# A new order of weight preparation at the hand-over from attention to the first expert layer

## The chip, the cores and the metric

One Trainium2 chip, one core. The metric is the device time of one execution in microseconds (us). The kernel before took 1001.23 us, the median of 3 runs (1000.52 to 1001.75). Its profile is of one more execution.

## The reference

Three layers run one after the other in float32.

```python
# attention: q, k, v are (4, 8, 576, 64); q and k are rotated first
scores = q_rot @ k_rot.T / sqrt(64)
attn = exp(scores - max); attn = attn / (sum(attn) + 1e-9)
x = (attn @ v).transpose(0, 2, 1, 3).reshape(2304, 512)
# first expert layer: w_in (512, 2048), w_out (2048, 512), float64
h = maximum(x @ w_in, 0)
x = (h * h) @ w_out
# second layer: 8 experts, each token goes to one
logits = x @ w_gate + modality_bias[modality_id]
e = argmax(logits); gate = softmax(logits)[e]
out = gate * (maximum(x @ w1[e], 0) @ w2[e])
```

## The kernel before

Every float32 matmul is done as three passes over a high and a low part of each operand. TensorE (PE) does the matmuls, VectorE (DVE), ScalarE (ACT) and GpSimd (POOL) make the parts, and SyncE (SP) issues all plain transfers, in order. Each engine carries out its instructions in the order in which the program lists them; an instruction that waits holds up all behind it on its engine.

Attention works on 16 pairs of heads. A table, `PLAN`, gives each step of a pair a due time, and the steps of all pairs are sorted by due time, 18 units further on per pair. A second table, `TAIL`, puts steps of the next layer into the same sorted list: the due times of that table are counted from the end of the 16th pair. The prefixes in `TAIL` name the steps: `wd` loads half a weight tile of the first expert layer (512 KB as 64-bit words) into one of 4 buffers `wraw`; `wx` (lines 518 to 520) takes its magnitude and turns its low words into floats on ACT; `wy` (524, 525) clamps and shifts on DVE; `wz` (529) merges both on POOL; `wb` (533) puts the sign back on DVE; `wh` (546) makes the high part on ACT; `wl` (549) makes the low part on POOL or DVE. The magnitude lives in one of 4 buffers of tag `t2`, named `wmag`. `xs0` to `xs3` load the first 512 tokens, `cl` and `setup` load the routing constants and prepare them (670 to 680).

The first expert layer goes over 5 blocks of up to 512 tokens, 16 slices of the hidden layer each, which makes 80 steps n. `m1` is the first matmul of a step (12 instructions at line 696, into a PSUM bank of tag `b`, of which there are 4). Then `re` (relu, 702) and `sq` (square, 706) run on ACT, `gg` and `gl` (710 and 714: the square again, and its low part) on DVE, and `m2` is the second matmul (12 instructions at line 730). `m1` runs two steps ahead of `m2`. Up to `m20` the order comes from `TAIL`; after it a loop over steps takes over. In block 0 the loop also prepares the other weights: `slot(i)` works on three half tiles at once, an even and an odd slot per step. An even half tile holds a slice of w_in, an odd one a slice of w_out. Weights stay in SBUF, so that blocks 1 to 4 prepare none. From block 1 on the logits are summed on DVE (`lg_dve`, line 742).

The tile `r` of relu comes from the tag `kr`, which has two buffers. In this kernel the first two tiles of that tag are `c_lt` and `wg_sb`, two of the routing constants.

Of the kernel before, what the change touches and what calls it, by code (L numbers as in the profile page):

```python
# [9 lines left out]
F32 = mybir.dt.float32  # L10
F32R = mybir.dt.float32r
BF16 = mybir.dt.bfloat16
I32 = mybir.dt.int32
# [8 lines left out]
B, H, S, D = 4, 8, 576, 64  # L22
NTOK, DM, DFF = B * S, H * D, 2048
E, EF = 8, 1024
# [10 lines left out]
def f32(ap):  # L35
    return ap.bitcast(F32)
# [129 lines left out]
}  # L166


# [316 lines left out]
class Weights:  # L485

    def __init__(self, nc, wio, pool):
        self.nc, self.wio, self.pool, self.extra, self.ring = nc, wio, pool, None, None
        self.w, self.raw, self.mag = {}, {}, {}

    def t2(self, shape, dt, name):
        return self.pool.tile(shape, dt, name=name, tag="t2", bufs=4)
# [37 lines left out]

    def sign(self, i):
        mag = self.mag[i]
        self.nc.vector.scalar_tensor_tensor(out=mag, in0=self.words(i)[:, :, 1], scalar=-2 ** 31, in1=mag,
                                            op0=ALU.bitwise_and, op1=ALU.bitwise_or)
        self.raw.pop(i)

# [15 lines left out]
def experts(tc, wts, ps, xT, rD, wexp, mod, wg, mb, cst, ident, yD, out):  # L552
    nc = tc.nc
    with ExitStack() as ctx:
# [3 lines left out]
        W, t2 = wts.w, wts.t2  # L558
# [4 lines left out]
        def kr(shape, dt, name):  # L563
            return sb.tile(shape, dt, name=name, tag="kr", bufs=2)

        def small(shape, dt, name):
            return sb.tile(shape, dt, name=name)
# [4 lines left out]
        xs, rs, gs, hs, yp, ysb, wgb, yts, tables = {}, {}, {}, {}, {}, {}, [], {}, {}  # L572
        raws, rbs = {}, {}

        def xload(b, ks):
            t0, n = BLOCKS[b]
            for k in ks:
                x = sb.tile([128, 2, n], F32R, name="xs", tag="xs", bufs=5)
                nc.sync.dma_start(out=f32(x), in_=xT[k, :, :, t0:t0 + n])
                xs[b, k] = x  # L580
# [45 lines left out]

        c_io8 = small([128, E], F32, "c_io8")
        c_io128 = small([128, 128], F32, "c_io128")
        c_lt = kr([128, 128], F32, "c_lt")
        c_id = small([128, NT], F32, "c_id")  # L630
        wg_sb = kr([128, 4, E], F32, "wg_sb")
        mb_sb = small([128, 2, E], F32, "mb_sb")
        mod_sb = small([128, NT, 2], I32, "mod_sb")

        def cload():
            o = 0
            for t, n in ((c_io8, E), (c_io128, 128), (c_lt, 128), (c_id, NT)):
                nc.sync.dma_start(out=t, in_=cst[:, o:o + n])
                o += n
            nc.sync.dma_start(out=wg_sb, in_=wg[0:DM].rearrange("(k p) e -> p k e", p=128))  # L640
            nc.sync.dma_start(out=mb_sb, in_=mb.rearrange("m e -> (m e)").partition_broadcast(128))
            nc.sync.dma_start(out=mod_sb, in_=mod.bitcast(I32).rearrange("(j p w) -> p j w", p=128, w=2))
# [24 lines left out]
        six = small([128, NCOL], I32, "six")  # L667

        def setup():
            nc.vector.tensor_copy(out=lt_b, in_=c_lt)  # L670
            nc.vector.memset(one_b, 1.0)
            nc.vector.memset(cum[:, 0], 0.0)
            nc.vector.tensor_copy(out=wg_s[:, :, 0:E], in_=wg_sb)
            nc.vector.tensor_tensor(out=wg_s[:, :, E:2 * E], in0=wg_sb, in1=f32(wg_s[:, :, 0:E]), op=ALU.subtract)
            nc.vector.tensor_copy(out=modf[:, 1], in_=mod_sb[:, :, 0])
            nc.vector.tensor_scalar(out=modf[:, 0], in0=modf[:, 1], scalar1=-1.0, scalar2=1.0, op0=ALU.mult, op1=ALU.add)
            for m, t in enumerate((bias, tmp3)):
                nc.vector.tensor_tensor(out=t, in0=modf[:, m].unsqueeze(2).to_broadcast([128, NT, E]),
                                        in1=mb_sb[:, m].unsqueeze(1).to_broadcast([128, NT, E]), op=ALU.mult)
            nc.vector.tensor_tensor(out=bias, in0=bias, in1=tmp3, op=ALU.add)  # L680
# [367 lines left out]
        pre, mid, post = {}, {}, {}  # L1048

        def at(d, n, *fs):  # L1050
            d.setdefault(n, []).extend(fs)
# [5 lines left out]
        for b in range(NB):  # L1057
            if b:
                q = NFC * b
                for k in range(4):  # L1060
                    if b == 1:
                        at((mid, pre)[k % 2], q - 6 + (k + 1) // 2, lambda b=b, k=k: xraw(b, k))
                        at(mid, q - 12 + k, lambda b=b, k=k: xrec(b, k))
                        e = nc.gpsimd if k < 2 else nc.vector
# [51 lines left out]
        def second(m):  # L1116
# [5 lines left out]
            if f == EFC - 1:  # L1122
                for t in ts:
                    finish(s, t)

        units = [(first, mm2, n) for n in range(N)] + [(emm1, second, m) for m in range(M0, M1)]
        yield dict(xs=lambda k: xload(0, [k]), cl=lambda _: cload(), setup=lambda _: setup(), m1=mm1, re=relu, sq=square,
                   gg=square_v, gl=rest, m2=mm2)
        wts.ring = ctx.enter_context(tc.tile_pool(name="w", bufs=1, reuse_waits="tile"))
        for q, (_, second_, n) in enumerate(units):  # L1130
            if q < NU - LA:
# [32 lines left out]
@with_exitstack  # L1164
def tile_attention_moe(ctx, tc, qx, kx, v, wio, wexp, mod, wg, mb, tabq, tabk, eye, cst, out):
    nc = tc.nc
    const = ctx.enter_context(tc.tile_pool(name="const", bufs=1))
    pool = ctx.enter_context(tc.tile_pool(name="wts", bufs=1))
    dram = ctx.enter_context(tc.tile_pool(name="scratch", bufs=1, space=DRAM))
    ident = const.tile([128, 128], F32, name="ident")  # L1170
    xT = dram.tile([4, 128, 2, NTOK], F32, name="xT")
    yD = dram.tile([NTOK, DM], F32, name="yD")
    rD = dram.tile([NP, 9, 128], F32, name="rD")
    wts = Weights(nc, wio, pool)
    ps = ctx.enter_context(tc.tile_pool(name="ps", bufs=1, space=PSUM))
    run = experts(tc, wts, ps, xT, rD, wexp, mod, wg, mb, cst, ident, yD, out)
    fs = dict(wd=wts.load, wx=wts.absolute, wy=wts.clamp, wz=wts.merge, wb=wts.sign, wh=wts.high)

    def tail(name, eng):
        if name == "open":  # L1180
            fs.update(next(run))
        elif name in fs:
            fs[name](0)
        elif name[0:2] == "wl":
            wts.low(int(name[2:]), nc.vector if eng == "V" else nc.gpsimd)
        else:
            fs[name[0:2]](int(name[2:]))

    with tc.manual_schedule():
        attention(tc, qx, kx, v, tabq, tabk, ident, eye, xT, rD, ps, tail)  # L1190
        next(run, None)
# [84 lines left out]
```

## Time and profile before

| | |
|---|---|
| time, median of 3 runs | 1001.23 us |
| time of the profiled execution | 998.48 us |
| its span, first to last instruction | 996.6 us |
| PE busy | 913.4 us (92% of the span) |
| DVE busy | 689.3 us |
| ACT busy | 532.3 us |
| POOL busy | 378.6 us |

Times of the trace are counted from the start of the span. Attention ends and the first expert layer begins at 317.69 us. A row of a timeline gives the start, the busy time (from the first to the last of the merged instructions), the engine, the line of the kernel, the operation, what it writes and reads, the count, and in brackets how long the engine had been idle before it and what ended the wait. SPq rows are transfers, from issue. [...]

### The profile page before, as it was taken

To read this page: it belongs to the slowest core of one execution; us is meant where nothing else is said; L and a number is where in the kernel's file an instruction comes from. 1 tells how busy PE (TensorE), PEld (TensorE's weight loads), DVE (VectorE), ACT (ScalarE), POOL (GpSimd) and SP (SyncE) were. 2 spreads that over 40 slices of the span, in tenths; PEclk is the share of its full clock that TensorE was granted. 3 is DMA by queue.
4 is the path that set the end of the run, shared out by engine and by line. 5 is a ranking of instruction groups with operands and counts; after the bars stand their busy time and mean duration, and the time that the engine had idled before them with its cause. 6 is when DMAs were issued, how large, how long until landed. Compare 5 with 4: busy or idle time off the path is not lost. (4 is left out here: it accounts for less than half of the span.)

```text
span 996.6 us, 15017 instructions
## 1 busy us (share of the span) xinstructions
PE 913.4 (92%) x5210; PEld 789.6 (79%) x5210; DVE 689.3 (69%) x1253; ACT 532.3 (53%) x1090; POOL 378.6 (38%) x292
## 2 busy tenths in 40 slices
PE   1888889999999598889999999999999999999996
PEld 0778888988888366668878887888888889999995
DVE  5889988989896699958555754665374766666650
ACT  3788888889897476631233223222434345555551
POOL 6778887878753466714001200200010123212011
PEclk9999999999999799999999999999999999999998
DMA  7556557565755445443003100300133258776630
GB/s 239 150 156 189 170 143 202 147 197 177 203 144 150 128 149 189 149 161 112 1 1 127 43 1 1 106 1 1 43 124 109 76 165 251 233 238 224 210 107 33
DMA packets 55714, 130.83 MB, mean 131 GB/s; under 512 B 11968, under 2 KB 16592, under 8 KB 55632
## 3 DMA queue, kind: packets, MB, share of 16 engines
q1 hardware_dynamic: 52592, 120.10, 39.6%
q0 software_dynamic: 3040, 9.70, 2.7%
q8 instruction: 43, 0.70, 0.3%
q14 instruction: 39, 0.32, 0.1%
HBM read 97.12 MB, written 19.21 MB: 117 GB/s over the span
## 5 line engine op out<-in xcount | busy, mean ns | idle before, releaser
L696 PE MATMUL h<-xs,w 128*128 128x512 f32 (+1 forms) x720 | 163.7, 373 | 9.7 <-POOL w L549 9.7
L702 ACT ACTIVATE r<-h 128x512 f32<-128x512 f32 (+1 forms) x80 | 44.4, 555 | 236.1 <-PE h L696 219.8
L696 PEld LDWEIGHTS h<-xs,w 128*128 128x128 f32 x720 | 125.5, 188 | 40.1 <-POOL w L549 14.1
L710 DVE SCALAR_TENSOR_TENSOR h<-h,r 128x512 f32<-128x512 f32 (+1 forms) x80 | 51.5, 644 | 125.2 <-ACT r L702 124.9
L730 PE MATMUL y<-w,gh 128*128 128x512 f32 x432 | 135.8, 396 | 0.0
L272 PE MATMUL sc<-kh,q 128*128 128x288 f32 (+2 forms) x336 | 98.5, 328 | 37.2 <-ACT kh L194 20.7
L288 ACT ACTIVATE e<-sc,nmx 128x576 f32<-128x576 f32 x144 | 107.0, 744 | 27.5 <-DVE nmx L277 27.1
L277 DVE TENSOR_REDUCE nmx<-sc 128x1 f32<-128x576 f32 x144 | 106.6, 750 | 17.2 <-PE sc L272 15.1
L967 DVE TENSOR_TENSOR w<-eraw,w 128x1024 fp32r<-128x1024 f32 x64 | 78.3, 1223 | 33.8 <-ACT w L966 33.6
L272 PEld LDWEIGHTS sc<-kh,q 128*128 128x128 f32 x336 | 62.7, 196 | 47.2 <-issue 24.1
L199 DVE TENSOR_TENSOR et<-b,et 128x512 fp32r<-128x512 f32 (+1 forms) x160 | 93.8, 624 | 8.0 <-ACT et L194 6.0
L330 PE MATMUL b<-ident,e 128*128 128x128 f32 x640 | 89.1, 277 | 9.6 <-DVE et L199 3.9
L730 PEld LDWEIGHTS y<-w,gh 128*128 128x128 f32 x432 | 80.2, 188 | 17.5
L272 PE MATMUL sc<-kl,q 128*128 128x288 f32 (+2 forms) x336 | 90.9, 305 | 0.0
L330 PEld LDWEIGHTS b<-ident,e 128*128 128x128 f32 x640 | 72.7, 141 | 18.3 <-PE b L321 5.2
L730 PE MATMUL y<-w,gl 128*128 128x512 f32 x216 | 84.9, 393 | 0.0
L194 ACT ACTIVATE et<-b 128x512 fp32r<-128x512 f32 (+1 forms) x160 | 82.7, 561 | 1.3 <-PE b L330 0.8
L364 PE MATMUL b<-et,vs 128*128 128x288 f32 x512 | 78.4, 295 | 0.1
L1012 PEld LDWEIGHTS h<-ye,w 128*128 128x128 f32 x576 | 75.1, 189 | 3.9
L615 POOL TENSOR_TENSOR xraw<-xraw,rbs 128x512 f32<-128x512 f32 (+1 forms) x12 | 15.7, 1310 | 159.6 <-DMA rbs<-xT 93.6
L1012 PE MATMUL h<-ye,w 128*128 128x256 f32 x576 | 76.3, 283 | 0.0
L1035 PE MATMUL y<-w,ge 128*128 128x512 f32 x288 | 75.3, 397 | 0.0
(216 smaller groups left out, 1832.4 us busy)
## 6 DMA issues: line engine op xcount, KB each, us to landing
eraw<-wexp SPq DMA_DIRECT2D x64, 512.0 KB, 3.5
wraw<-wio SPq DMA_DIRECT2D x32, 512.0 KB, 4.0
rawq<-qx SPq DMA_DIRECT2D x15, 576.0 KB, 5.0
rawk<-kx SPq DMA_DIRECT2D x15, 576.0 KB, 6.5
xT<-xo SPq DMA_DIRECT2D x24, 288.0 KB, 6.1
kh<-kh SPq DMA_DIRECT2D x45, 144.0 KB, 2.3
vraw<-v SPq DMA_DIRECT2D x16, 320.0 KB, 6.3
q<-ql SPq DMA_DIRECT2D x32, 144.0 KB, 3.9
```

Of the source, the lines that this page charges most:

```text
L194: nc.scalar.activation(out=out, in_=in_, func=ACTF.Copy)
L199: on[eng].tensor_tensor(out=out, in0=in0, in1=f32(hi), op=ALU.subtract)
L272: nc.tensor.matmul(out=o[:, x:x + w], lhsT=q[:, hd, q0:q0 + 128], rhs=k[:, hd, y:y + w], start=(n == 0), stop=(n == len(ops) - 1))
L277: nc.vector.tensor_reduce(out=m, in_=sc(p, j)[:, :, 0:HS], axis=AX.XY, op=ALU.max, negate=True)
L288: nc.scalar.activation(out=e(p)[:, o:o + S].rearrange("p (a b) -> p a b", a=2), in_=sc(p, j)[:, :, 0:HS], func=ACTF.Exp, bias=live[p, f"nm ...
L330: nc.tensor.transpose(t[:, i * 128:(i + 1) * 128], x[:, o:o + 128], ident)
L364: nc.tensor.matmul(out=o, lhsT=lhsT.rearrange("p a b -> p (a b)"), rhs=rhs, start=(c == 0 and i == 0), stop=(c == 4 and i == 1))
L696: nc.tensor.matmul(out=h, lhsT=w[:, a, k * 128:(k + 1) * 128], rhs=xs[b, k][:, c], start=(k == 0 and i == 0), stop=(k == 3 and i == 2))
L730: nc.tensor.matmul(out=yp[t], lhsT=g[a][:, t * 128:(t + 1) * 128], rhs=w[:, c, 512:1024], start=(f == 0 and i == 0), stop=(f == NFC - 1 an ...
L967: nc.vector.tensor_tensor(out=w[:, 1], in0=r, in1=f32(w[:, 0]), op=ALU.subtract)
L1012: nc.tensor.matmul(out=h, lhsT=w[:, a, k * 128:(k + 1) * 128], rhs=x[:, c], start=(k == 0 and i == 0), stop=(k == 3 and i == 2))
L1035: nc.tensor.matmul(out=yp[s, t], lhsT=g[a][:, t * 128:(t + 1) * 128], rhs=w[:, c, 512:1024], start=(f == 0 and i == 0), stop=(f == EFC - 1 ...
```

## The change

Three things change. The due times of the second half of `TAIL` are new, `wl4` to `wl7` move from POOL to DVE, and `m10` to `m20` with what follows each of them are interleaved with the weight steps. The loading and the preparation of the routing constants leave `TAIL` for steps 13 and 17 of the loop; `c_lt` and `wg_sb` now lie in one buffer of tag `t2` instead of two of tag `kr`. And in the loop the sign step of an odd half tile writes into a PSUM bank of tag `b`, which its high and low parts then read.

```diff
@@ TAIL @@
...
-    "wd6": (-138.181, "D"), "wl1": (-93.230, "P"), "wd7": (-88.464, "D"), "xs0": (-84.177, "D"),
...
-    "m10": (1204.840, "T"), "m11": (1293.864, "T"), "re0": (1305.121, "A"), "wh7": (1325.671, "A"),
...
+    "wd6": (-138.181, "D"), "wz4": (-103.400, "P"), "wl1": (-101.000, "P"), "wl2": (-100.500, "P"),
...
+    "wy8": (-70.950, "V"), "wz8": (-70.940, "P"), "m10": (-70.930, "T"), "m11": (-70.920, "T"), "re0": (-70.910, "A"),
...
@@ class Weights @@
     def sign(self, i):
         mag = self.mag[i]
-        self.nc.vector.scalar_tensor_tensor(out=mag, in0=self.words(i)[:, :, 1], scalar=-2 ** 31, in1=mag,
+        if self.bank and i % 2:
+            self.mag[i] = self.bank([128, 512], "wbank").bitcast(I32)
+        self.nc.vector.scalar_tensor_tensor(out=self.mag[i], in0=self.words(i)[:, :, 1], scalar=-2 ** 31, in1=mag,
                                             op0=ALU.bitwise_and, op1=ALU.bitwise_or)
@@ experts @@
-        c_lt = kr([128, 128], F32, "c_lt")
...
-        wg_sb = kr([128, 4, E], F32, "wg_sb")
...
+        passing = []
...
         def cload():
-            o = 0
+            o, t = 0, t2([128, 160], F32, "c_t")
+            c_lt, wg_sb = passing[:] = t[:, 0:128], t[:, 128:160].rearrange("p (k e) -> p k e", e=E)
...
         def setup():
+            c_lt, wg_sb = passing
...
+        at(mid, 13, cload)
+        at(mid, 17, setup)
-        yield dict(xs=lambda k: xload(0, [k]), cl=lambda _: cload(), setup=lambda _: setup(), m1=mm1, re=relu, sq=square,
-                   gg=square_v, gl=rest, m2=mm2)
+        yield dict(xs=lambda k: xload(0, [k]), m1=mm1, re=relu, sq=square, gg=square_v, gl=rest, m2=mm2)
+        wts.bank = bank
```

Before, on ACT, from the last evacuation of attention (`xo`) to the first relu (`r`); the words in brackets name the queues or engines that a row waits for:

```order
L194 ACTIVATE xo<-b 128x288 [waits PE_49] x2
L519 ACTIVATE wmag<-wraw 128x512 [waits Pool_49]
L520 ACTIVATE wraw<-wraw 128x512
L546 ACTIVATE wf<-wmag 128x512 [waits DVE_49] x2
L519 ACTIVATE wmag<-wraw 128x512 [waits DMAHW6_49,Activation_49,Pool_49]
L520 ACTIVATE wraw<-wraw 128x512
L519 ACTIVATE wmag<-wraw 128x512 [waits DMAHW7_49,Pool_49]
L520 ACTIVATE wraw<-wraw 128x512
L519 ACTIVATE wmag<-wraw 128x512 [waits DMAHW0_49,Pool_49]
L520 ACTIVATE wraw<-wraw 128x512
L702 ACTIVATE r<-h 128x512 [waits DMAHW2_49,DVE_49,PE_49]
```

After, the same stretch on ACT (line numbers from 530 on are 2 or 3 higher):

```order
L548 ACTIVATE wf<-wmag 128x512
L194 ACTIVATE xo<-b 128x288 [waits PE_49]
L519 ACTIVATE wmag<-wraw 128x512 [waits DMAHW5_49,Pool_49]
L520 ACTIVATE wraw<-wraw 128x512
L194 ACTIVATE xo<-b 128x288 [waits PE_49]
L548 ACTIVATE we<-wmag 128x512 [waits DVE_49,Activation_49]
L519 ACTIVATE wmag<-wraw 128x512 [waits DMAHW7_49,Activation_49]
L520 ACTIVATE wraw<-wraw 128x512
L705 ACTIVATE r<-h 128x512 [waits PE_49]
L709 ACTIVATE gh<-r 128x512 [waits Activation_49]
L548 ACTIVATE we<-wmag 128x512 [waits DVE_49]
```

Of the three magnitude pairs that stood between the last `xo` and the first relu, `wx7`, `wx8` and `wx9`, one is left there (`wx8`); the relu waits for PE alone and no longer for a DMA queue and DVE.

Before, on SP, from the last sums of attention (`rD`) to the first weight load of the new layer:

```order
L305 DMA rD<-rs 9x128 [waits DMAHW5_49,Activation_49]
L391 DMA xT<-xo 64x2x576 [waits DMAHW6_49,Activation_49]
L391 DMA xT<-xo 64x2x576 [waits DMAHW7_49]
L638 DMA c_io_3981<-cst 128x8 [waits DMAHW0_49]
L638 DMA c_io_3982<-cst 128x128 [waits DMAHW1_49]
L638 DMA c_lt<-cst 128x128 [waits DMAHW2_49]
L638 DMA c_id<-cst 128x18 [waits DMAHW3_49]
L640 DMA wg_sb<-wg 128x4x8 [waits DMAHW4_49]
L641 DMA mb_sb<-mb 128x16 [waits DMAHW5_49]
L642 DMA mod_sb<-mod 128x18x2 [waits DMAHW6_49]
L496 DMA wraw<-wio 128x512 [waits DMAHW7_49,DVE_49]
```

After, SP from one store of sums earlier:

```order
L305 DMA rD<-rs 9x128 [waits Activation_49]
L496 DMA wraw<-wio 128x512 [waits DMAHW7_49,DVE_49,Pool_49]
L496 DMA wraw<-wio 128x512 [waits DMAHW0_49,DVE_49]
L391 DMA xT<-xo 64x2x576 [waits DMAHW1_49,Activation_49]
L391 DMA xT<-xo 64x2x576 [waits DMAHW2_49]
L581 DMA xs<-xT 128x2x512 [waits DMAHW3_49,PE_49]
L581 DMA xs<-xT 128x2x512 [waits DMAHW4_49,DVE_49,PE_49]
L581 DMA xs<-xT 128x2x512 [waits DMAHW5_49]
L581 DMA xs<-xT 128x2x512 [waits DMAHW6_49]
L305 DMA rD<-rs 9x128 [waits DMAHW7_49,Activation_49]
L496 DMA wraw<-wio 128x512 [waits DMAHW0_49,DVE_49]
```

Two weight loads, `wd8` and `wd9`, now stand ahead of the token loads `xs`, where before they stood behind seven loads of constants.

Before, on DVE, one step of block 0:

```order
L710 SCALAR_TENSOR_TENSOR h<-h,r 128x512 [waits Activation_49]
L714 TENSOR_TENSOR gl<-h,gh 128x512 [waits DVE_49,PE_49,Activation_49]
L524 TENSOR_SCALAR wmag<-wmag 128x512 [waits Activation_49]
L525 TENSOR_SCALAR wmag<-wmag 128x512 [waits DVE_49]
L533 SCALAR_TENSOR_TENSOR wmag<-wraw,wmag 128x512 [waits DMAHW1_49,Pool_49]
L549 TENSOR_TENSOR w<-wmag,w 128x512 [waits Activation_49]
L524 TENSOR_SCALAR wmag<-wmag 128x512 [waits Activation_49]
L525 TENSOR_SCALAR wmag<-wmag 128x512 [waits DVE_49]
L533 SCALAR_TENSOR_TENSOR wmag<-wraw,wmag 128x512 [waits DMAHW2_49,Pool_49]
```

After, the same step:

```order
L713 SCALAR_TENSOR_TENSOR h<-h,r 128x512 [waits Activation_49]
L717 TENSOR_TENSOR gl<-h,gh 128x512 [waits DVE_49,PE_49,Activation_49]
L524 TENSOR_SCALAR wmag<-wmag 128x512 [waits Activation_49]
L525 TENSOR_SCALAR wmag<-wmag 128x512 [waits DVE_49]
L535 SCALAR_TENSOR_TENSOR wmag<-wraw,wmag 128x512 [waits DMAHW0_49,Pool_49]
L551 TENSOR_TENSOR w<-wbank,w 128x512 [waits DMAHW4_49,DMAHW2_49,Activation_49]
L524 TENSOR_SCALAR wmag<-wmag 128x512 [waits Activation_49]
L525 TENSOR_SCALAR wmag<-wmag 128x512 [waits DVE_49]
L535 SCALAR_TENSOR_TENSOR wbank<-wraw,wmag 128x512 [waits DMAHW1_49,Pool_49]
```

The order of the step is as before; the second sign writes `wbank`, a PSUM bank, and the low part of an odd half tile reads it there.

## Rows read from the trace of the kernel before

**Rows 1.** Busy time by stretch: length, engines, granted clock, DMA share, GB/s
```profile
335.00:340.00 5.00, 1.74 (x3) 1.00 (x4) 4.76 (x13) 4.51 (x9) 2.81 (x3) 0.50 0.30 105
...
430.00:440.00 10.00, 8.15 (x30) 6.57 (x31) 4.86 (x8) 1.66 (x3) 0.00 (x0) 0.83 0.53 210
```

**Rows 2.** Timeline of PE at the hand-over, columns as told above
```profile
317.69 6.27 PE L696 MATMUL h<-xs,wf 128*128 128x512 f32 x26
...
337.07 1.22 PE L730 MATMUL y<-wf,gh 128*128 128x512 f32 x2 [9.95 <-ACT gh L706]
...
343.31 2.92 PE L696 MATMUL h<-xs,we 128*128 128x512 f32 x12
```

**Rows 3.** Timeline of ACT, end of attention and hand-over
```profile
300.62 0.74 ACT L288 ACTIVATE e<-sc,nmx 128x576 f32<-128x576 f32 x1 [0.91 <-DVE nmx L277]
...
329.63 0.66 ACT L519 ACTIVATE wmag<-wraw 128x512 f32<-128x512 f32 x1 [5.57 <-DMA wraw<-wio]
...
335.38 0.60 ACT L702 ACTIVATE r<-h 128x512 f32<-128x512 f32 x1 [3.28 <-issue]
```

**Rows 4.** Timeline of DVE at the hand-over
```profile
333.99 1.30 DVE L670 CAST lt_b<-c_lt 128x128 bf16<-128x128 f32 x1
...
337.95 0.69 DVE L710 SCALAR_TENSOR_TENSOR h<-h,r 128x512 f32<-128x512 f32 x1
```

**Rows 5.** Timeline of SP's transfers at the hand-over
```profile
319.63 1.85 SPq L638 DMA_DIRECT2D c_io<-cst  x2
...
324.06 26.11 SPq L496 DMA_DIRECT2D wraw<-wio  x7
```

**Rows 6.** Timeline of DVE in block 1
```profile
447.76 0.70 DVE L710 SCALAR_TENSOR_TENSOR h<-h,r 128x512 f32<-128x512 f32 x1 [4.03 <-ACT r L702]
...
449.20 0.69 DVE L742 SCALAR_TENSOR_TENSOR junk<-ysb,wgb 128x512 f32<-128x512 f32 x1
...
458.83 0.70 DVE L710 SCALAR_TENSOR_TENSOR h<-h,r 128x512 f32<-128x512 f32 x1 [1.11 <-ACT r L702]
```

**Rows 7.** Timeline of PE in block 0, rows with a wait
```profile
355.43 2.60 PE L696 MATMUL h<-xs,w 128*128 128x512 f32 x10 [0.37 <-POOL w L549]
...
362.30 2.60 PE L696 MATMUL h<-xs,w 128*128 128x512 f32 x10 [1.07 <-POOL w L549]
...
417.25 2.60 PE L696 MATMUL h<-xs,w 128*128 128x512 f32 x10 [1.04 <-POOL w L549]
431.85 4.12 PE L696 MATMUL h<-xs,wf 128*128 128x512 f32 x11 [3.40 <-DVE xs L625]
```

**Rows 8.** Timeline of DVE in block 0, from one step
```profile
361.19 1.34 DVE L524 TENSOR_SCALAR wmag<-wmag 128x512 f32<-128x512 f32 x1
...
363.50 1.81 DVE L549 TENSOR_TENSOR w<-wmag,w 128x512 fp32r<-128x512 f32 x1
365.24 0.41 DVE L524 TENSOR_SCALAR wmag<-wmag 128x512 f32<-128x512 f32 x1
```

**Rows 9.** By line, DVE: ns minimum/median/maximum of one, first and last start, forms
```profile
L199 DVE TENSOR_TENSOR et<-b,et x160: 408/679/693, 33.6 to 313.3; 128x512 fp32r<-128x512 f32 x128, 128x256 fp32r<-128x256 f32 x32
...
L199 DVE TENSOR_TENSOR ql<-rawq,q x16: 749/759/1742, 13.7 to 285.3; 128x576 fp32r<-128x576 f32 x16
...
L549 DVE TENSOR_TENSOR w<-wmag,w x12: 1710/1802/1808, 349.7 to 423.3; 128x512 fp32r<-128x512 f32 x12
...
L533 DVE SCALAR_TENSOR_TENSOR wmag<-wraw,wmag x32: 673/685/1785, 17.6 to 420.2; 128x512 int32<-128x512 int32 x32
```

**Rows 10.** Timeline of POOL in the same step
```profile
360.99 1.26 POOL L549 TENSOR_TENSOR w<-wmag,w 128x512 fp32r<-128x512 f32 x1
363.12 1.64 POOL L529 TENSOR_TENSOR wmag<-wmag,wraw 128x512 int32<-128x512 int32 x1 [0.88 <-ACT wmag L519]
366.34 1.55 POOL L529 TENSOR_TENSOR wmag<-wmag,wraw 128x512 int32<-128x512 int32 x1 [1.58 <-ACT gh L706]
```

**Rows 11.** Busy tenths of POOL in 40 slices of 24.9 us
```profile
POOL 6778887878753466714001200200010123212011
```

More of the change, by code (lines that the diff above doesn't have):

```diff
@@ L487, in __init__ @@
     def __init__(self, nc, wio, pool):
-        self.nc, self.wio, self.pool, self.extra, self.ring = nc, wio, pool, None, None
+        self.nc, self.wio, self.pool, self.extra, self.ring, self.bank = nc, wio, pool, None, None, None
         self.w, self.raw, self.mag = {}, {}, {}
```

24 rows, old and new, of the table TAIL are left out of this document.

## The prediction

> **What bounds the kernel now.** I read busy time by stretch first, because PE is busy for 92% of the span and so the time is PE's work plus PE's gaps. The gaps that the change can reach lie between 317 and 432 us. [...] The first matmuls of steps 0, 1 and 2 begin at 317.69, and the second matmul of step 0 at 337.07, after 9.95 us of waiting for `gh` on ACT [rows 2]. `gh` follows the first relu, and the timeline of ACT says why that is late. ACT waits 5.57 us for a weight load before 329.63, takes two magnitude pairs until 332.1 (335.38 - 3.28), and then stands for 3.28 us until the relu at 335.38 [rows 3]. The profile names no releaser for those 3.28 us, but the order does: the relu's tile needs the buffer of `c_lt`, which `setup` reads on DVE at 333.99, with a cast that ends at 335.29 [rows 4]. The weight load was late because it was issued at 324.06, behind seven loads of constants that began at 319.63 [rows 5].
>
> The second loss is the rest of block 0. There PE's own work for a step is 5.54 us: in block 1, where nothing holds it, `gg` comes at 447.76 and, two steps on, at 458.83 [rows 6], so a matmul of 512 columns costs 5.54/24 = 0.231 us. In block 0 the waits for POOL's low part recur every 6.87 us, nine times from 355.43 to 417.25 [rows 7]. The third is the end of block 0: 3.40 us of waiting for the split tokens at 431.85, and then 11 matmuls in 4.12 us, where 10 took 2.60 before [rows 7], at a mean clock of 0.83 [rows 1].
>
> **The hand-over.** What must stand before the second matmul of step 0 in the new order? PE runs three first matmuls, 36 x 0.231 = 8.3 us, so it asks for `gl` of step 0 at 317.7 + 8.3 = 326.0. The relu can start when 12 matmuls are through, at about 320.7. ACT has after the last `xo` of attention one high part and one magnitude pair, 0.6 + 1.3 = 1.9 us by a length of about 0.66 for each of the three [rows 3], and so is free when PE is. `wd8`, for which that pair waits, is now issued once `wb4` is through, at about 301 us in place of 324.06, so the load is not what is late. On DVE three low parts, two signs and three clamp pairs stand between the last `et` (begins at 313.3, ends at 313.9 [rows 9]) and `gg`: 3 x 0.68 + 2 x 0.69 + 3 x 0.86 = 6.0 us, by the lengths without a lock: 749 ns for 576 columns makes 0.68 for 512, a sign takes 685 ns [rows 9], a clamp pair twice 0.43, as its first half takes 0.41 [rows 8]. The waits between them add about 2.9: DVE stands until 317.0 for a high part that ACT makes only after an `xo`, and then twice for a merge of POOL (1.3 us after its clamp). So `gg` comes at 322.8 and, after 2 x 0.69, `gl` ends at 324.2, 1.8 us before PE asks. Should each of the five instructions with two SBUF inputs be held by POOL for the full 1.1 us by which 1802 exceeds 679 [rows 9], without any of it lying in those waits, `gl` would come 313.9 + 6.0 + 5.5 + 1.4 = 326.8, a wait of 0.8. So I take no gap and no fall of the clock.
>
> What it costs at the end of attention: one magnitude pair (1.3) and one high part (0.6) move on ACT to between the last exponentials. ACT has 0.91 us of idle time before the exponential at 300.62 [rows 3]; about 0.4 of the pair and after it a little remain uncovered. I take 0.4 us, between 0 (all covered) and 1.9 (nothing covered). DVE gets one sign, one clamp pair and one more sign there, 2.2 us, into waits for scores that are about as long.
>
> The first matmul of step 3 then begins at 317.69 + 0.4 + 48 x 0.231 = 329.2 instead of 343.31 [rows 2]: **14.1 us less**. On SP, `wd8` and `wd9` stand ahead of the token loads, but wait only for signs that, by the order, DVE reaches at about 301 and 305 us; the token loads after the first wait for the last transposes in any case.
>
> **Block 0.** The two uneven lengths of line 524 (1.34 and 0.41) and the 1.81 of line 549 [rows 8] read beside POOL's rows: POOL's low part ends at 360.99 + 1.26 = 362.25, the clamp at 362.53; POOL's merge ends at 364.76, DVE's low part at 365.31 [rows 8, 10]. DVE's instruction stands until POOL's is through. One with an operand in PSUM does not: 160 of `et<-b`, from 33 to 314 us, where POOL is busy for 50 to 80% of most slices [rows 11], took 693 ns at most, while `ql`, all in SBUF, reached 1742 [rows 9]. So the odd low part from PSUM takes 0.68 in place of 1.80. Not all of the 1.12 us is won. The clamp after it would start at 364.1, when POOL's merge still runs until 364.76, and end 0.28 later as the other clamp does, at 365.04 instead of 365.65: 0.61 is left. POOL's next merge follows that clamp (366.34), and the low part for which PE waits follows that merge, so the step shrinks from 6.87 to 6.26 us, still above PE's 5.54. Over ten steps, **6.1 us**.
>
> [...]
>
> The sign that now writes PSUM keeps two SBUF inputs. Its bounds are 0.69, as `junk`, which also writes PSUM from two SBUF inputs [rows 6], and 1.785, a sign held by POOL [rows 9]. In the step it ran before POOL's merge began, and its place does not change, so I take 0.69; at 1.785 the step would be 6.26 + 1.1 = 7.4 and block 0 lose 10 x 0.5 = 5 us instead.
>
> At the end of block 0, DVE's last odd low part is shorter and every instruction behind it earlier; following the locks of DVE and POOL through the token sums I get the first split 1.1 us nearer to PE's demand, 3.5 to 2.4 us of wait. The slow matmuls behind the wait cost 4.12 - 11 x 0.26 = 1.3 us; a shorter wait may spare them or not. Between 1.1 and 2.4, I take **2.0**.
>
> **The constants.** `setup` on DVE took from 333.99 to 337.95 at the most, 4.0 us [rows 4], in steps that now leave 1.11 us idle each [rows 6]; `gl` is wanted two steps, some 9 us, after it can be made, which hides it. Without that cover it costs up to 4.0 - 1.1 = 2.9 us. The loads at step 13 stand behind the last weight load and ahead of loads that are used three steps later: nothing.
>
> **Sum.** 14.1 + 6.1 + 2.0 = 22.2 us. The profiled execution took 998.48, so 976.3 for one like it; it lies 2.75 below the median of the runs shown, and I predict from that median: 1001.2 - 22.2 = **979.0 us**.
>
> **Rivals.** *The clamp is not held (0.15).* If DVE gets its second clamp in before POOL, the whole 1.12 us is won: a step of 5.75, 11.2 us over ten steps, and DVE comes to the end of block 0 far enough ahead to spare 3.5 there: 14.1 + 11.2 + 3.5 = 28.8, **972.4 us**. For it: the order of the two is decided by fractions of a microsecond. Against it: the other clamp is held in every step.
>
> *The gap returns in part (0.20).* The relu or `gg` of step 0 is late once more, now behind weight work in its own queue: the new order puts seven weight steps of three engines, each waiting for the one before, into the 7 us from 313.9 to 321. If they lag by 6.5 us, PE waits some 4.6 us and pays 1.3 for the clock, as at 431.85: 6 us of the 22 are lost, **985 us**. For it: before, DVE's queue of the same kind kept `setup` waiting until 333.99 [rows 4]. Against it: the loads are early.
>
> *PSUM banks run short (0.05).* Each step of the loop now takes two of the four banks. If the first matmul of a step had to wait for the odd low part of the step just before, PE, ACT and DVE would run in series: 2 x 2.77 on PE, and between them relu, square, high part and low part, 0.6 + 0.6 + 0.6 + 0.7, with the magnitude pair of 1.3 in ACT's queue, 9.3 us a step, 2.5 more than 6.87 over 14 steps, 35 us; less the 14.1 of the hand-over, 21 slower: **1022 us**. Against it: by the order the bank is that of the low part two steps back, which ended at 365.31 in the step whose POOL part came at 369.1. It decides only where this low part slips by more than 3.3 us, and it outweighs the hand-over from 8 us a step.
>
> *The change does not reach PE (0.02).* The waits move but their sum stays: 1001.
>
> **How the numbers follow.** The forecast has 0.58. Its own range is 974 to 984: the attention end (up to 1.5 more), the sign (rarely held), and the end of block 0 (0.9 less to 0.4 more), with the runs' own spread of about 1 us. The range of 8 in 10 reaches to both neighbours, 971 to 988. A measurement of this kernel can tell about 0.2% (2 us) from no change. Faster: 0.58 + 0.15 + 0.20 = 0.93; the same 0.02; slower 0.05.
>
> **What would show it.** In the timeline of PE, the second matmul of step 0 directly behind the first matmuls, at about 326.5, no idle row over 1 us there, and a granted clock of 1.00 from 325 to 345 us. On ACT the first relu at about 321. In block 0, `w<-wbank` on DVE at 0.68, one clamp of 1.34 and one of some 0.9 us in a step, waits of PE every 6.26 us. `setup` near step 17 with no wait of PE behind it. It is wrong if PE waits over 2 us before step 3, if the period in block 0 is 6.87 or below 5.8, or if first matmuls wait for DVE's `w<-wbank`.

## The result, and the profile after

The changed kernel takes 978.5 us (median of 4 runs, 977.67 to 979.24) where the kernel before takes 1001.48 us beside it: a ratio of 0.9772, with an interval of 0.9755 to 0.9789. The prediction was 979.0 us. The span of the profiled execution falls from 996.6 to 977.3 us, and PE's busy time hardly at all (913.4 to 911.8 us): what went is idle time of PE.

The timeline of PE in the kernel after, at the hand-over, answers to [rows 2]. Its columns are start, length, engine, line, operation and count.

```profile
318.53 0.42 PE L364 MATMUL b<-rk,vs 128*128 128x288 f32 x2
318.79 8.56 PE L699 MATMUL h<-xs,wf 128*128 128x512 f32 x36
327.19 0.63 PE L733 MATMUL y<-wf,gh 128*128 128x512 f32 x2
...
329.95 2.90 PE L699 MATMUL h<-xs,we 128*128 128x512 f32 x12
```

The wait of 9.95 us is gone; step 3 begins at 329.95 instead of 343.31 us. ACT and DVE in the same stretch (answering to [rows 3, 4]) show how early the operands now are:

```profile
321.79 0.60 ACT L705 ACTIVATE r<-h 128x512 f32<-128x512 f32 x1 [0.64 <-PE h L699]
```

```profile
323.36 0.69 DVE L713 SCALAR_TENSOR_TENSOR h<-h,r 128x512 f32<-128x512 f32 x1
324.15 0.69 DVE L717 TENSOR_TENSOR gl<-h,gh 128x512 fp32r<-128x512 f32 x1
```

The first relu waits for PE alone, and `gl` of step 0 ends at 324.84 (324.15 + 0.69), 2.35 us before PE begins the second matmul at 327.19 (its first two instructions there read `gh`; the one with `gl` begins at 327.65). The windows of the kernel after, for the two stretches of [rows 1] (the second shifted to the same work), and two finer ones behind the wait of 2.42 us:

```profile
335.00:340.00 5.00, 5.00 (x23) 4.06 (x22) 4.68 (x10) 3.92 (x8) 3.05 (x2) 1.00 0.35 107
410.00:420.00 10.00, 8.25 (x29) 6.66 (x30) 4.76 (x8) 1.56 (x3) 0.00 (x0) 0.83 0.61 210
411.75:414.00 2.25, 2.25 (x5) 1.82 (x6) 1.75 (x3) 0.00 (x0) 0.00 (x0) 0.50 0.57 146
414.00:416.30 2.30, 2.30 (x9) 1.83 (x8) 0.00 (x0) 0.18 (x1) 0.00 (x0) 0.77 0.95 317
```

PE is full, at a granted clock of 1.00 (full speed), where it had 1.74 of 5 us at 0.50. The end of block 0 has not changed its character: PE, idle for 2.42 us, starts again at 0.50.

One step of block 0 on DVE in the kernel after (before: [rows 8]), POOL's merge in the same step (before: [rows 10]), and PE's waits in two steps (before: [rows 7]):

```profile
371.80 1.41 DVE L524 TENSOR_SCALAR wmag<-wmag 128x512 f32<-128x512 f32 x1
373.25 0.43 DVE L525 TENSOR_SCALAR wmag<-wmag 128x512 int32<-128x512 int32 x1
373.60 0.68 DVE L535 SCALAR_TENSOR_TENSOR wmag<-wraw,wmag 128x512 int32<-128x512 int32 x1
374.20 0.68 DVE L551 TENSOR_TENSOR w<-wbank,w 128x512 fp32r<-128x512 f32 x1
374.80 0.94 DVE L524 TENSOR_SCALAR wmag<-wmag 128x512 f32<-128x512 f32 x1
375.77 0.43 DVE L525 TENSOR_SCALAR wmag<-wmag 128x512 int32<-128x512 int32 x1
376.12 0.69 DVE L535 SCALAR_TENSOR_TENSOR wbank<-wraw,wmag 128x512 int32<-128x512 int32 x1
```

```profile
373.91 1.54 POOL L529 TENSOR_TENSOR wmag<-wmag,wraw 128x512 int32<-128x512 int32 x1 [0.98 <-DVE wmag L525]
```

```profile
372.99 2.60 PE L699 MATMUL h<-xs,w 128*128 128x512 f32 x10 [0.52 <-POOL w L551]
...
379.28 2.60 PE L699 MATMUL h<-xs,w 128*128 128x512 f32 x10 [0.43 <-POOL w L551]
```

The odd low part takes 0.68 instead of 1.80 us, and the clamp behind it 0.94 instead of 0.41, because it now meets POOL's merge (which ends at 375.45, the clamp at 375.74). The step is 6.31 us ((397.09 - 346.61)/8), before 6.87; the nine waits are 0.43 to 0.52 us instead of 1.0 to 1.1.

Last, set-up on DVE at its new place, and PE behind it:

```profile
438.02 1.36 DVE L681 TENSOR_TENSOR bias<-modf,mb_sb 128x144 f32<-128x144 f32 x1
...
440.68 0.69 DVE L717 TENSOR_TENSOR gl<-h,gh 128x512 fp32r<-128x512 f32 x1
```

```profile
437.91 1.29 POOL L621 TENSOR_TENSOR xraw<-xraw,rbs 128x512 f32<-128x512 f32 x1 [2.69 <-DMA rbs<-rD]
```

```profile
441.43 3.07 PE L699 MATMUL h<-xs,w 128*128 128x512 f32 x12 [0.33 <-DVE gl L717]
```

It was not free: one of its multiplications took 1.36 us, as it stood behind POOL (the second takes 0.30). `gl`, that of step 20, came late, and PE's next first matmul, that of step 21, waited for it: the loop issues set-up in its step 17, when PE is already at the first matmuls of steps 19 and 20.

**Stage by stage.** The parts of the program before 290 us and behind step 22 are the same in all kernels, but their lengths differ between executions (the first between 288.8 and 292.6 us, the second between 530.2 and 532.0), so I compare distances within a trace. The landmarks are POOL's last but one `vs` of attention (line 199, at 289.40 us before; the last one begins at 305.72) and the start of the first matmul of steps 0, 3, 15, 17 and 22 (before: 317.69, 343.31, 422.46, 438.57 and 466.34). Each column is the difference of two starts in us; the last goes to the end of the span. The other kernels are those of the experiments.

| kernel | vs to 0 | 0 to 3 | 3 to 15 | 15 to 17 | 17 to 22 | 22 to end |
|---|---|---|---|---|---|---|
| before | 28.29 | 25.62 | 79.15 | 16.11 | 27.77 | 530.26 |
| before2 | 28.32 | 25.88 | 79.16 | 16.30 | 27.83 | 532.01 |
| after | 28.72 | 11.16 | 73.42 | 15.31 | 28.38 | 530.24 |
| after2 | 28.71 | 12.08 | 73.47 | 13.81 | 27.98 | 530.46 |
| a_nobank | 28.71 | 12.27 | 79.18 | 16.41 | 27.83 | 530.28 |
| b_bank | 28.29 | 26.20 | 74.22 | 15.35 | 27.80 | 531.77 |
| b_const | 28.28 | 19.86 | 79.79 | 16.38 | 28.53 | 530.35 |
| b_own | 28.29 | 27.47 | 79.98 | 16.39 | 27.89 | 531.48 |
| c_order | 28.70 | 12.19 | 73.70 | 15.38 | 27.82 | 530.70 |
| a_oddps | 28.73 | 12.19 | 69.68 | 13.35 | 29.17 | 530.36 |
| a_split | 28.73 | 12.01 | 73.42 | 12.37 | 27.78 | 530.62 |
| a_best | 28.73 | 11.56 | 69.67 | 11.89 | 27.78 | 531.72 |
| a_both | 28.72 | 12.06 | 67.57 | 11.93 | 27.80 | 531.71 |

### The profile page after: what moved, and what is told of

Same layout as the page of the kernel before. It is cut to its first block, busy times and chain, and to the rows that moved or that the text cites. A ratio compares the mean times of both kernels' runs of the same rounds, so it can differ in the third digit from the quotient of the medians.

```text
span 977.3 us, 15032 instructions
## 1 busy us (share of the span) xinstructions
PE 911.8 (93%) x5210; PEld 789.5 (81%) x5210; DVE 677.9 (69%) x1257; ACT 530.6 (54%) x1090; POOL 369.9 (38%) x288
## 5 line engine op out<-in xcount | busy, mean ns | idle before, releaser
L1045 POOL DMA_INDIRECT out<-ob,six x19 | 22.5, 1184 | 140.7 <-ACT ob L1044 109.3
```

## The experiments

### Is it PSUM that shortens block 0?

a_nobank is the kernel after without the one line that hands over the banks; b_bank is the kernel before with the sign into PSUM and nothing else.

```diff
-        wts.bank = bank
```

> The kernel after, but with every sign left in SBUF (the new order and the moved constants stay). My theory: the PSUM sign alone carries block 0, and the hand-over is carried by the rest. The first matmul of step 3 stays at 329.5 to 330.5 us; the odd low part is again 1.80 us, the step 6.87 us, nine waits of about 1.05 us; the wait at the end of block 0 returns to about 3.4 us. Time: 978.5 + 9 x 0.57 + 1.0 = 984.6 us (983 to 987). Rival, the phase: the new order alone shifts POOL and DVE against each other so that the step is short without PSUM; then the step stays at 6.3 us and the time at 978 to 980 us.

> The kernel before, with the odd signs written to PSUM and nothing else. My theory: the terms add, so the gap at the hand-over stays (second matmul of step 0 at about 337 us), the odd low part takes 0.68 us, the step 6.3 us, the wait at the end of block 0 about 2.4 us. Time: 1001.5 - 9 x 0.57 - 1.0 = 995.3 us (993 to 997). Rival, the phase: the short step needs the new order; then it stays near 6.87 us and the time at 1000 to 1002 us.

Measured: a_nobank 987.18 us, 0.9859 of before (0.984 to 0.9879); b_bank 995.48 us, 0.9942 (0.9926 to 0.9959). PE in a_nobank, in a step and at the end of block 0:

```profile
371.19 2.60 PE L699 MATMUL h<-xs,w 128*128 128x512 f32 x10 [1.04 <-POOL w L551]
...
420.19 4.00 PE L699 MATMUL h<-xs,wf 128*128 128x512 f32 x11 [3.42 <-DVE xs L627]
```

The steps stand where my theory put them, in both orders: steps 3 to 15 take 79.2 us without PSUM and 73.4 to 74.2 with it. The rival of the phase is out. The time of a_nobank lies 0.2 us above my range.

### Constants or order: what closed the gap?

b_const takes only the constants out of the old order. b_own leaves them there and only gives them tiles outside the relu's ring. c_order puts them back into the new order.

```diff
 # b_own
-        c_lt = kr([128, 128], F32, "c_lt")
+        c_lt = k2([128, 128], F32, "c_lt")
...
-        wg_sb = kr([128, 4, E], F32, "wg_sb")
+        wg_sb = small([128, 4, E], F32, "wg_sb")
 # c_order, in TAIL and in experts
...
+    "cl": (-78.475, "D"), "wx8": (-70.990, "A"), "wl6": (-70.980, "V"), "wb7": (-70.970, "V"), "wd11": (-70.960, "D"),
...
+    "sq0": (-70.900, "A"), "setup": (-70.895, "V"), "gg0": (-70.890, "V"), "gl0": (-70.880, "V"), "wh7": (-70.870, "A"), "m12": (-70.860, "T"),
...
+        c_lt = kr([128, 128], F32, "c_lt")
+        wg_sb = kr([128, 4, E], F32, "wg_sb")
...
```

> The kernel before, with the constants alone moved (loads at step 13, set-up at step 17, their tile out of the relu's ring); the old order of the weight steps stays. My theory: the hand-over has two causes of like size. Without seven loads of constants ahead of it the weight load is issued at 319.6 instead of 324.06 us, ACT's two last magnitude pairs end at about 327.7, the sign on DVE at 329.7, gh at about 331, so PE starts its second matmul at 331.3 instead of 337.07 and, with the clock fallen, step 3 at about 335.7 instead of 343.31: 7.6 us less, 0.3 back for set-up at step 17. Time 994 us (992 to 997). Rival 1, the order is all: the relu is late behind weight work anyway, 1000 to 1002 us. Rival 2, the constants are all: the gap closes without the new order, 987 to 989 us.

> The kernel before, with c_lt and wg_sb in tiles of their own in place of the two-buffer ring that the relu's output uses; loads and set-up stay where they are. My theory: the 3.28 us for which the relu stands is then gone (relu at about 332.1), but the time is not, because set-up still stands on DVE until 337.95 ahead of gg, and PE then waits for gl instead: step 3 at 343 us as before, time 1000.5 to 1002 us. Rival, the buffer is the cost: what the relu gains PE gains, 3.3 us or, with the clock, up to 4.6: 997 to 998 us.

> The kernel after, with the constants put back into the hand-over (loads ahead of the relu of step 0 in SP's order, set-up on DVE directly ahead of gg of step 0, c_lt and wg_sb in the relu's two-buffer ring); the new order and the PSUM sign stay. It completes the square of old and new order with the constants inside and outside. In the kernel before, moving the constants out alone took 5.8 us off the hand-over. Theory 1, the two causes overlap: in the new order the loads come early enough, set-up takes 2.9 to 4 us on DVE ahead of gl of step 0, which had 2.3 us to spare, so PE waits 0.6 to 1.6 us there, and step 17 is free of its 0.6: 978 to 981 us. Theory 2, the causes add: the constants cost about 5.8 us in this order too, 983 to 985 us.

Measured: b_const 996.61 us, 0.9955 (0.994 to 0.997); b_own 1003.16 us, 1.0024 (1.0012 to 1.0035); c_order 979.75 us, 0.9792 (0.9778 to 0.9806). PE and DVE in b_const:

```profile
330.97 0.74 PE L731 MATMUL y<-wf,gh 128*128 128x512 f32 x2 [3.12 <-ACT gh L707]
333.82 0.79 PE L731 MATMUL y<-wf,gl 128*128 128x512 f32 x1 [2.11 <-DVE gl L715]
```

```profile
330.32 1.44 DVE L525 TENSOR_SCALAR wmag<-wmag 128x512 int32<-128x512 int32 x1
331.68 0.68 DVE L533 SCALAR_TENSOR_TENSOR wmag<-wraw,wmag 128x512 int32<-128x512 int32 x1
332.28 0.69 DVE L711 SCALAR_TENSOR_TENSOR h<-h,r 128x512 f32<-128x512 f32 x1
```

`gh` came when I said (331 us), but `gg` did not: in the old order two clamps and two signs stand ahead of it on DVE, and half a clamp (line 525) is held by POOL (1.44 us). The gap shrinks by 5.8 us, not 7.6, and the rest needs the order. b_own is the plainest case of a wait that takes another's place:

```profile
334.44 1.22 PE L730 MATMUL y<-wf,gh 128*128 128x512 f32 x2 [5.88 <-ACT gh L706]
341.13 0.80 PE L730 MATMUL y<-wf,gl 128*128 128x512 f32 x1 [5.47 <-DVE gl L714]
```

```profile
336.14 1.10 DVE L673 CAST wg_s<-wg_sb 128x32 fp32r<-128x32 f32 x1
...
337.27 1.19 DVE L674 TENSOR_TENSOR wg_s<-wg_sb,wg_s 128x32 fp32r<-128x32 f32 x1
...
339.59 0.69 DVE L710 SCALAR_TENSOR_TENSOR h<-h,r 128x512 f32<-128x512 f32 x1
```

The relu is 2.6 us earlier, and all of it goes into the wait for `gl`. The kernel is even 2 us slower, outside the 1000.5 to 1002 us that I had given. Of that 0.9 us is set-up: the earlier relu lets ACT finish a high part earlier, POOL's low parts then run into set-up (335.94 to 338.42), and a cast and a subtraction of 128x32 take 1.1 and 1.2 us (in before 0.17 and 0.19); set-up takes 4.84 us (334.75 to 339.59) where it took 3.96 [rows 4]. The rest lies mostly in a granted clock that stays low for longer (0.50 from 342 to 344 us, in before 0.86): the 12 first matmuls of step 3 take 3.72 us, in before 2.92. In b_bank, which does not touch the hand-over, they take 3.77, so this part may belong to the execution and not to the change. In c_order the same set-up, with the relu again waiting for it, is hidden:

```profile
322.06 0.22 DVE L672 CAST lt_b<-c_lt 128x128 bf16<-128x128 f32 x1
...
325.78 0.69 DVE L716 TENSOR_TENSOR gl<-h,gh 128x512 fp32r<-128x512 f32 x1
```

```profile
322.36 0.60 ACT L704 ACTIVATE r<-h 128x512 f32<-128x512 f32 x1 [2.49 <-DVE lt_b L672]
```

```profile
326.94 0.62 PE L732 MATMUL y<-wf,gh 128*128 128x512 f32 x2
```

`gl` ends at 326.47 and PE begins its second matmul at 326.94. So the two causes overlap (theory 1): in the new order the constants cost nothing that the traces can tell where they stood (12.19 us beside 11.16 and 12.08), in the old one 5.8. What in the new order does it, the earlier weight loads, the interleaving, or `wl4` to `wl7` on DVE, no run takes apart.

### What holds the clamp?

```diff
 # in absolute(i)
-        nc.scalar.activation(out=f32(mag), in_=f32(x[:, :, 1]), func=ACTF.Abs)
+        self.top[i] = f32(mag)
+        if self.bank and i % 2:
+            self.top[i] = self.out[i] = self.bank([128, 512], "wbank")
+        nc.scalar.activation(out=self.top[i], in_=f32(x[:, :, 1]), func=ACTF.Abs)
...
 # in clamp(i)
-        nc.vector.tensor_scalar(out=f32(mag), in0=f32(mag), scalar1=W_MIN, scalar2=W_MAX, op0=ALU.max, op1=ALU.min)
+        nc.vector.tensor_scalar(out=f32(mag), in0=self.top.pop(i), scalar1=W_MIN, scalar2=W_MAX, op0=ALU.max,
+                                op1=ALU.min)
...
```

> The kernel after, with the magnitude of an odd weight slot written by ACT into the PSUM bank that its sign uses later, so that the odd clamp on DVE reads PSUM and no longer SBUF alone. My theory: it is POOL's instruction in SBUF that holds the odd clamp (1.36 us instead of 0.41). Read from PSUM it takes about 0.69 us beside POOL; the merge behind it starts at the end of POOL's low part, and by the rows of the step after (0.69 + 0.35 + 0.60 + 0.60 on DVE, then the even clamp held until the merge ends, then 1.55 + 1.30 on POOL) the POOL cycle is 5.4 us, under PE's 5.54: the step becomes 5.55 to 5.65 us, PE's waits for POOL's low part go to nearly nothing. Time 978.5 - 9 x 0.7 = 972.2 us (970.5 to 974). Rival 1, the clamp waits for something else, or an input in PSUM is held as well: step 6.3, time 978 to 980. Rival 2, the bank that is now taken earlier makes ACT or the first matmuls wait: 980 us or more.

Measured 976.27 us, 0.9739 (0.9725 to 0.9754). A step in a_oddps, on DVE and on POOL:

```profile
379.31 0.68 DVE L527 TENSOR_SCALAR wmag<-wbank 128x512 f32<-128x512 f32 x1
380.02 0.66 DVE L529 TENSOR_SCALAR wmag<-wmag 128x512 int32<-128x512 int32 x1
...
381.81 0.95 DVE L527 TENSOR_SCALAR wmag<-wmag 128x512 f32<-128x512 f32 x1
```

```profile
379.11 1.29 POOL L556 TENSOR_TENSOR w<-wmag,w 128x512 fp32r<-128x512 f32 x1
```

The mechanism is right: while POOL's low part runs (379.11 to 380.40), the clamp from PSUM takes 0.68 us, 681 ns in the mean of nine, where from SBUF it took 1.35 to 1.41 in after. The size was not, and the time lies above the 974 us at which my range ended: the hold moves on to the shift behind the clamp (0.66 instead of 0.43), the other clamp keeps its 0.95, DVE has hardly any idle time left (busy for 50.2 of 52 us from 345 to 397), and the step is 5.86, not 5.6. Of the 3.7 us won in block 0, 1.0 is lost at set-up, which costs 1.4 us here. Both rivals are out.

### The end of block 0

The tokens of block 1 are loaded, summed and scaled on POOL and DVE (`xraw`), and then split into a high part (ACT) and a low part (DVE), `xs`, for which PE waits there.

```diff
         def first(n):
-            for f in (mm1, relu, square, square_v, rest):
+            mm1(n)
+            if n == NFC - 1:
+                for k in range(4):
+                    xsplit(1, k)
+            for f in (relu, square, square_v, rest):
                 f(n)
...
-                    at(mid, q - 3, lambda b=b, k=k: xsplit(b, k))
+                    if b > 1:
+                        at(mid, q - 3, lambda b=b, k=k: xsplit(b, k))
```

> The kernel after, with the four splits of block 1's tokens put on ACT and DVE directly behind the last first-matmul of block 0, ahead of the relu, gg and gl of that step. My theory: gg and gl (1.43 us) are all that stands on DVE between the token sums and the first split; the wait of PE falls from 2.42 to about 1.0 us and the stretch of slow matmuls behind it (11 in 4.33 us) becomes shorter or goes. From step 15 to step 17 12.3 to 13.9 us in place of 15.31. Time 978.5 - 1.4 to 3.0, about 976.3 us. Rival: the token sums, not their place behind gg, are what is late (POOL's last one ends at 408.4 us), so PE starts earlier but its matmuls are paced by the splits and the end does not move: 978 to 979 us.

Measured 976.92 us, 0.9758 (0.9742 to 0.9773). PE in a_split:

```profile
410.78 2.83 PE L699 MATMUL h<-xs,wf 128*128 128x512 f32 x11 [0.99 <-DVE xs L627]
```

The wait is 0.99 us and the clock does not fall (1.00 from 410 to 420 us): steps 15 to 17 take 12.37 us, the low end of what I wrote. The 11 matmuls take 2.83 us, so they are not paced by the splits, and the rival is out. `gg` and `gl` ahead of the splits were the cause that could be moved. That is worth 1.4 us, the difference to after2 below, where the clock does not fall either; the times alone can't tell a_split from after (0.9742 to 0.9773 and 0.9755 to 0.9789).

### Versions that beat both, and the repeats

a_best joins the last two edits and puts set-up at step 15; a_both adds the even magnitude in PSUM (three of four banks a step).

```diff
-        at(mid, 17, setup)
+        at(mid, 15, setup)
 # a_both, in absolute(i)
+        elif self.bank:
+            self.top[i] = self.bank([128, 512], "wabs")
```

> The kernel after with both edits, the odd magnitude in PSUM and the early splits, and with set-up at step 15, where DVE stands idle for about 4 us, instead of step 17, where it cost PE 0.6 us. My theory: the terms add, 978.5 - 6.3 - 2.2 - 0.6 = 969.4 us (967.5 to 971.5). Rival: PE comes to the end of block 0 earlier by 6 us and then waits there for the token sums, whose POOL and DVE work is not shorter, so that part of the 6 comes back: 972 to 975 us.

> The kernel a_best with the even magnitude in a PSUM bank as well, so that a step of block 0 takes three of the four banks instead of two. DVE was without idle time in a step of 5.86 us there, with the even clamp at 0.94 us, held by POOL's merge. My theory: it takes 0.68, the step 5.6 us (PE's own work is 5.54), time 974.0 - 10 x 0.25 = 971.5 us (970.5 to 973). Rival, the banks run short: a first matmul, or ACT's magnitude, waits for a bank that DVE has not released, the step stays at 5.86 us or grows: 974 us or more.

Measured: a_best 973.98 us, 0.9714 (0.9698 to 0.9729); a_both 970.85 us, 0.97 (0.9686 to 0.9713). The time of a_best lies where its rival had put it, but the rival's mechanism is out: PE waits only 0.48 us at the end of block 0, and set-up costs nothing. In the stages it gains 6.9 us against the mean of the two traces of after, while its time falls by 4.5: in its trace the parts outside the stages are longer, the tail by 1.4 us (531.72) and the stretch ahead of `vs` by 1.2 (290.85), and both differ as much between two executions of one kernel. In a_both the even clamp takes 0.68:

```profile
382.54 0.67 DVE L529 TENSOR_SCALAR wmag<-wabs 128x512 f32<-128x512 f32 x1
```

```profile
380.32 0.61 PE L706 MATMUL h<-xs,w 128*128 128x512 f32 x2
381.18 2.60 PE L706 MATMUL h<-xs,w 128*128 128x512 f32 x10 [0.25 <-POOL w L558]
```

The step is 5.66 us ((391.96 - 346.65)/8) where PE's own work is 5.54, and one short wait is left, for POOL; no matmul waits for a bank. This is the fastest version, 7.65 us under the kernel after.

> The kernel before once more, unchanged, for a second profile. The profiled execution of before took 998.48 us, 2.7 below the median of its timed runs. If that was jitter in parts that the change does not touch, this one shows the hand-over (first matmul of step 0 to that of step 3, 25.62 us), block 0 (steps 3 to 15, 79.15 us) and the end of block 0 (steps 15 to 17, 16.11 us) within 0.7 us of the first, and the difference before 318 us and behind 467 us.

> The kernel after once more, unchanged, for a second profile. The parts that the change touches should repeat: from the last subtraction of the values on POOL to the first matmul of step 0 28.7 us, steps 0 to 3 11.2 to 12.3 us, steps 3 to 15 73.4, steps 15 to 17 15.3, and step 20 to 21 5.55 plus what set-up costs (0.5 in the first profile).

before2 took 1002.5 us, after2 977.57. The touched stages repeat within 0.3 us in before; of the 4 us between the two executions of before, 1.7 lie ahead of 290 us and 1.75 behind step 22. after2 differs from after in two places: token loads land later (0 to 3 takes 0.9 more, with a wait of 0.34 us for one of them), and at the end of block 0 the clock does not fall, behind the same wait:

```profile
411.75:414.00 2.25, 2.17 (x9) 1.80 (x10) 1.84 (x4) 0.00 (x0) 0.00 (x0) 1.00 0.45 158
```

## Why the prediction was right, step by step

**The hand-over** (14.1): by the means of the two traces each, steps 0 to 3 lose 14.1 us and attention's end costs 0.41, so 13.7. The cost at the end of attention was put at 0.4. Of the seven traces with the new order and the constants outside, after has the shortest steps 0 to 3 (11.16 to 12.27 us, 11.9 in the mean); by their mean the hand-over gains 13.4. `gl` was predicted for 324.2 and ended at 324.84 with the whole hand-over 1.1 us later than I had it, of which 0.67 had come up ahead of 290 us. The causes I read (the relu behind `c_lt`'s buffer, the weight load behind the constants) were real, but the runs add what I had not said: they are not a sum. Freeing the buffer alone gains nothing (b_own), taking the constants out alone brings 5.8, the new order brings 13 with the constants left in.

**Block 0** (6.1): 5.7. The odd low part is 0.68 us in all twelve, the sign 0.69, the clamp behind it held, all as said; the step is 6.31 instead of 6.26. The tile's rows in the kernel after show that the upper bound for the sign was no fancy either:

```profile
L535 DVE SCALAR_TENSOR_TENSOR wbank<-wraw,wmag x12: 690/693/1779, 330.4 to 400.7; 128x512 int32<-128x512 int32 x12
L551 DVE TENSOR_TENSOR w<-wbank,w x12: 680/683/685, 336.4 to 403.8; 128x512 fp32r<-128x512 f32 x12
```

One of twelve met POOL and took 1.78 us: the last one, at 400.7. The sign at that place was held in the kernel before too (1.78 us at 420.19), so the change did not bring this. In the kernel after, POOL's low part ran at that place from 400.61 to 401.90 us; the sign, which keeps two SBUF inputs though it writes PSUM, was held. The low part from PSUM took 0.685 us at most in all twelve, and the clamp from PSUM 0.68 beside POOL (a_oddps).

**The end of block 0** (2.0): the wait fell to 2.42 us as worked out (2.4); the open question, whether the slow matmuls stay, has two answers. They stayed in after (11 in 4.33 us, a gain of 0.9 against the mean of before) and went in after2 (2.83 us, a gain of 2.4). The value taken lies between.

**The constants** (0): this term was wrong, and by its cover. It costs 0.4 us in the mean of after and after2. I had `gl` hidden because its product comes two steps later. But PE waits for it sooner, and not for its value: in block 1 a step takes three banks for `junk` and one for `h` out of a ring of four, so the next step's first matmul needs the very bank that this step's `gl` gives back. In the step two further on `gl` ends at 452.22, 0.4 us before PE's next start at 452.63:

```profile
451.53 0.69 DVE L717 TENSOR_TENSOR gl<-h,gh 128x512 fp32r<-128x512 f32 x1
```

That is all the slack there is, and set-up, with one instruction held by POOL, used it up (`gl` ends at 441.37, PE starts at 441.43). Set-up costs 0.6 us in after, 0.7 in b_const and 1.4 in a_oddps, where an instruction of it took 1.27 to 1.42 us beside POOL (in a_oddps behind a `junk` of 1.63); 0.2 in after2, where only a `junk` ahead of it was held (1.62); nothing in a_nobank and a_split, where all of set-up ran free. So it depends on where POOL stands. At step 15, where there is no `junk` yet, it costs nothing (a_best, a_both). The rival of the banks was sought in block 0; its mechanism was at work here.

**The sum**: 13.7 + 5.7 + 1.65 - 0.4 = 20.7 us by the profiles, 22.2 predicted, 22.98 by the medians. That the median came out within 0.5 us is partly luck: the terms were too large by 1.5 us, and about 2.3 us of the measured gain lie in none of the touched stages. The two traces of each kernel show 1.4 us of that ahead of 290 us and behind step 22, where single executions of one kernel differ as much; whether it belongs to the change stays open. **The rivals**: the second clamp was held in every step, no gap returned at the hand-over, and in block 0 PSUM banks did not run short even at three a step.

## What to carry to other kernels

When an engine stands still, list everything that would still be late if its cause were gone: of two causes in series, taking one away can give nothing (b_own) or less than its wait (b_const), and an order that leaves slack (2.35 us here) hides even what was the cause before (c_order). If an instruction is stretched by another engine, find out which operand makes it wait: moving that operand to PSUM shortened it (the odd low part from 1.80 to 0.68 us) where moving the output did not (a held sign took 1.78 us either way), and what was won moved the hold on to the next instruction until DVE was busy nearly all the time. When work is put into an idle slot, its cover is the first instruction that waits for anything behind it, a buffer that it returns included, not the one that uses its value.

## What the runs showed of the hardware that was not expected

Behind nearly the same idle time of PE, 2.36 to 2.43 us, the granted clock fell to 0.50 in after, where it was still below full speed from 414 to 416.3 us (0.77), and stayed at 1.00 in after2; the 11 matmuls there took 4.33 and 2.83 us. They took 3.92 and 4.13 in c_order and b_bank, behind 2.36 and 2.43 us. Behind 1.91 us (a_oddps) and less they took 2.84 at most. What decides it no run shows.

A clamp of one SBUF input took 0.41 us by itself, 0.94 beside POOL's merge and 1.36 beside its low part; from PSUM it took 0.68 by itself (a_oddps, at 338.54) and beside POOL. The form that is slower alone was the faster one here. What I had not expected is that the shift behind it, 0.43 us before, then took 0.64 to 0.71 in its place.
